# An attention and mixture-of-experts kernel: logits summed from PSUM, rows of x evicted without them

## The chip, the cores and the metric

The kernel runs on one core of a Trainium2 chip. The metric is the device time of one execution in microseconds (us), as the median of several runs. PE is TensorE (PEld its weight loads), DVE is VectorE, ACT is ScalarE, POOL is GpSimd, SP is the engine whose queue issues most DMAs.

## The reference

Attention over 8 batches, 12 heads, 448 tokens and 64 values a head, with the heads mixed before and after the softmax, and behind it a layer of 8 experts (FF = 1024), of which each token takes one:

```python
scores = scale * np.matmul(q, k.transpose(0, 1, 3, 2))
scores = np.einsum('bhij,hg->bgij', scores, w_pre)
scores = scores - np.max(scores, axis=-1, keepdims=True)
attn = np.exp(scores)
attn = attn / (np.sum(attn, axis=-1, keepdims=True) + 1e-09)
attn = np.einsum('bhij,hg->bgij', attn, w_post)
out = np.matmul(attn, v)                 # -> x, 3584 tokens x 768

logits = x @ w_gate                      # 3584 x 8
expert_idx = np.argmax(logits, axis=1)
# gate_w: the chosen expert's softmax probability
for e in range(E):
    h = np.maximum(x[expert_idx == e] @ w1[e], 0.0)
    out[expert_idx == e] = gate_w * (h @ w2[e])
```

## The kernel before, in words

**Tiles and steps.** The 448 queries of a batch are four tiles T of 120, 120, 120 and 88; there are 32 tiles. A tile is cut into blocks of 20 queries, six for a tile of 120 and five for one of 88, so a batch has 23 blocks and the program 184. The attention stage is a loop over the blocks. One turn is called a step here. What stands in a step is a table: `at(u, stage, what)` puts a piece of work into step u, and `ORDER` (L772) is the order of the stages within a step. Nothing else reorders it: each engine takes its instructions in the order in which the program is written. Waits between engines are put in by the framework wherever two instructions touch the same tile of SBUF or the same PSUM bank and one engine has to wait for the other.

**A step.** `mix` (L301) multiplies a block's scores with the heads' mixing matrix into the two banks `bm`. `maxima` (L307, DVE) takes the row maxima of both, `powers` (L315, ACT) the exponentials and their sums, one bank after the other. In the next step `recip` (L323, L325) and `weigh` (L332, POOL) scale the second mixing matrix, and two steps on `post` (L348) and `evict_p` (L366, L360) make the mixed, transposed attention. Scores of later tiles (`qk` L268, `evict_s` L278) are computed in between, into `bs0` and `bs1`, two tiles of two banks each, and are laid out anew by DMAs on SP (`relayout`, L288, into `sb`), two steps ahead of their `mix`. On ACT there are also the roundings of queries (`split_q`, L146) and of key chunks of the next batch (`split_k`, L120).

**The end of a tile.** When all blocks of a tile are mixed, `av` (L388, L408) multiplies with v. `rows` (L428) turns the result into rows of tokens: for each half of the heads, three matmuls against `xg`, whose 136 columns are an identity (128) and the 8 columns of `w_gate` that belong to those 128 values. The outcome is 120 tokens x 3 x 136 values in one bank of `bs1`: 128 values of x and 8 partial logits, three times. The second half fills the other bank. In the next step `evict_r` (L435, ACT) copies both to `XR` in SBUF. One step later `choose` (L455) sums the six partial logits of each expert from `XR` and takes the largest (L459, L460), and `store_x` (L442) writes the rows to `XD` in DRAM, in two halves. Then `mark`, `rank`, `gate` (L500), `place` (L507 to L519) and `scatter` put the token into its expert's list.

**Where these steps stand.** Counted from a batch's first step as 0, `evict_r` stands in the steps 2, 8, 14 and 20, for the tile whose `rows` were in the step before; key chunks of the next batch are rounded in the steps 8, 10, 12, 14, 16 and 18 of the first seven batches. `place` of the tile before stands in the same steps as `evict_r`, on DVE, in the stage "vec". In `ORDER` "vec" comes behind "recip" and ahead of "evict_r", "early" (the key chunk) and "max".

**The last tiles.** For tiles 30 and 31 the same pieces are written out by hand (L839 to L915), together with the gathering of the first expert's tokens from `XD`. Then come the experts, `hidden` (L1065) and `result` (L1086), over sorted tokens.

Of the kernel before, what the change touches and what calls it, by code (L numbers as in the profile page):

```python
# [8 lines left out]
F32 = mybir.dt.float32  # L9
# [6 lines left out]
AX = mybir.AxisListType  # L16
# [4 lines left out]
HD = H * D  # L21
NT = B * S
NE, FF = 8, 1024
P = 128
IT = 120
# [7 lines left out]
NPAIR = H // 2  # L33
CAP = 512
XG = P + NE
NTILE = B * 4
# [8 lines left out]
def attn_moe_kernel(ctx, tc, qT, kT, v, w_pre, w_post, w_gate, w1, w2, out):  # L45
    nc = tc.nc
# [4 lines left out]
    XD = dram.tile([NT + 1, HD], F32, name="XD")  # L51
# [6 lines left out]
    geom = []  # L58
    for T in range(NTILE):
        it = T % 4  # L60
        ni = min(IT, S - it * IT)
# [25 lines left out]
    sm_p = att.enter_context(tc.tile_pool(name="smp", bufs=4))  # L87
    pt_p = att.enter_context(tc.tile_pool(name="ptp", bufs=2))
    x_p = att.enter_context(tc.tile_pool(name="xp", bufs=1))
# [5 lines left out]
    bank_s = [ps_s.tile([P, 2, 512], F32, name=f"bs{n}") for n in range(2)]  # L95
# [275 lines left out]
    HOME, SIDE, SHEET = {}, {}, {}  # L371
# [49 lines left out]
    XR, LG, DD = {}, {}, {}  # L421
# [9 lines left out]
    def evict_r(T, g):  # L431
        ni = geom[T][2]
        if g == 0:
            XR[T] = x_p.tile([IT, NPAIR, XG], F32, name="xr", bufs=2)
        nc.scalar.copy(out=XR[T][:ni, 3 * g:3 * g + 3, :], in_=SHEET.pop((T, g)))  # L435

    def store_x(T, halves=(0, 1)):
        b, it, ni = geom[T][:3]
        t0 = b * S + it * IT
        for n in halves:  # L440
            cs = slice(3 * n, 3 * n + 3)
            nc.sync.dma_start(  # L442
                out=XD[1 + t0:1 + t0 + ni, n * HD // 2:(n + 1) * HD // 2].rearrange("t (c x) -> t c x", x=P),
                in_=XR[T][:ni, cs, :P])

    state = {"base": base0}
    RK = slice(0, NE), slice(NE, 2 * NE)
# [3 lines left out]

    def choose(T):
        b, it, ni = geom[T][:3]
        lg = sm_p.tile([IT, NE], F32, name="lgs")
        nc.vector.reduce_sum(out=lg[:ni], in_=XR[T][:ni, :, P:XG].rearrange("p c e -> p e c"),  # L455
                             axis=AX.X)
        m8 = sm_p.tile([IT, NE], F32, name="m8")
        i8 = sm_p.tile([IT, NE], U32, name="i8")
        nc.vector.max(out=m8[:ni], in_=lg[:ni])  # L459
        nc.vector.max_index(out=i8[:ni], in_max=m8[:ni], in_values=lg[:ni])  # L460
        DD[T] = (lg, m8, i8)
# [150 lines left out]
    def turn(sl, banks, T=None):  # L612
        for ks, bank in zip(KS, banks):
            for n, k in enumerate(range(ks.start, ks.stop)):
                nc.tensor.matmul(out=bank[:, n * P:(n + 1) * P],  # L615
                                 lhsT=XX["s"][:, sl, k * P:(k + 1) * P], rhs=ident,
                                 start=(T is None or n == 0), stop=(T is None), is_transpose=True)
        if T is None:
            return
        ni, hit = geom[T][2], XX["hit", T][:, (sl - 2) * P:(sl - 1) * P]  # L620
        for ks, bank in zip(KS, banks):
            for n, k in enumerate(range(ks.start, ks.stop)):
                nc.tensor.matmul(out=bank[:, n * P:(n + 1) * P], lhsT=XR[T][:ni, k, :P],
                                 rhs=hit[:ni], start=False, stop=(k == ks.stop - 1))

    def split_x(sl, banks):
# [38 lines left out]
    def at(u, stage, *what):  # L665
        steps.setdefault((u, stage), []).append(what)
# [13 lines left out]
    for T in range(NTILE):  # L680
        u0, n = ustart[T], len(geom[T][3])
# [8 lines left out]
    for T in range(NTILE):  # L690
        b, it, ni = geom[T][:3]
        u0, n = ustart[T], len(geom[T][3])
        if T > 1:
            up = ustart[T - 2]
            at(up, "load", load_q, T)
            for part in range(2):
                at(up + 1 + 2 * part, "split", split_q, T, part)
        for g in range(3):
            for c in (2 * g, 2 * g + 1):
                if (T, g) in qsteps:  # L700
                    at(qsteps[T, g], "qk", qk, T, c)
                    at(qsteps[T, g], "evict_s", evict_s, T, c)
        if it == 0 and b + 1 < B:
            U = ustart[T + 4]
            for part, k in enumerate((16, 17, 19, 20, 22, 24, 25, 27)):
                at(u0 + k, "load", load_v, b + 1, part)
            for c in range(NPAIR):
                at(U - 18 + 2 * c, "load", load_k, b + 1, c)
                at(U - 15 + 2 * c, "early", split_k, b + 1, c)
        if T + 1 == NTILE:  # L710
            continue
        vs, r = vsteps[T], rsteps[T]
        for groups in ((0, 1),) if vs[0] == vs[1] else ((0,), (1,)):
            at(vs[groups[0]], "av", av_side, T, groups)
            at(vs[groups[0]], "av", av, T, groups)
        for g in range(2):
            at(vs[g], "side", evict_side, T, g)
            at(vs[g] + 1, "vec", evict_x, T, g)
            at(r, "rows", rows, T, g, bank_s[1][:, g, :])
            at(r + 1, "evict_r", evict_r, T, g)  # L720
        near = T + 2 - NTILE
        if near == 0:
            continue
        for n in range(2):
            at(r + 2 + n, "store", store_x, T, (n,))
        if T == EDGE - 2:
            at(r + 2, "choose", choose, T)
            at(r + 2, "choose", mark, T)
            at(r + 3, "rank", rank, T)
            at(r + 3, "gate", gate, T)  # L730
            for do in (place, token, number):
                at(r + 4, "vec", do, T)
            at(r + 5, "scatter", scatter, T)
            continue
        if T == EDGE - 1:
            at(r + 1, "choose", choose, T)
            at(r + 1, "choose", mark, T)
            at(r + 2, "relayout", rank, T)
            at(r + 2, "relayout", gate, T)
            for do in (place, token, number):  # L740
                at(r + 2, "vec", do, T)
            at(r + 2, "early", scatter, T)
            continue
        long = T + 2 < NTILE and len(geom[T + 2][3]) > 5
        at(r + (1 if near == 0 else 2), "choose", choose, T)
        at(r + (1 if near == 0 else 4 if long else 2), "choose", mark, T)
        u = r + 2 if near == 0 else r + 3 if near == -1 else rsteps[T + 1]
        at(u, "rank", rank, T)
        at(u, "gate", gate, T)
        at(u + 1, "vec", place, T)  # L750
        w = 1 if T == LAST else 4 if T + 3 < NTILE and len(geom[T + 3][3]) > 5 else 2
        at(u + w, "token", token, T)
        at(u + w + 1, "number", number, T)
        at(u + w + 1, "scatter", scatter, T)
# [20 lines left out]
    vec, act = nc.vector.tensor_copy, nc.scalar.copy  # L775
# [60 lines left out]
    T = NTILE - 1  # L836
# [6 lines left out]
    nc.vector.memset(bank_m[0][JC:, W3], 0.0)  # L843
    run(NU, "evict_r")
    store_x(T - 1)
    choose(T - 1)
    mark(T - 1)
# [3 lines left out]
    post(*final, banks=bank_m)  # L851
    rank(T - 1)
    turn(0, side)
    run(NU, "evict_p")
    evict_p(*final, banks=bank_m)
# [23 lines left out]
    logits(T, 0)  # L879
    rows(T, 0, bank_s[1][:, 0, :])  # L880
    evict_r(T, 0)
    logits(T, 1)
    choose_at_once(T)
    mark(T)
    rows(T, 1, bank_s[1][:, 1, :])
    evict_r(T, 1)
    rank(T)
    gate(T)
    turn(1, side)
    place(T)  # L890
    store_x(T)
    nslot = const.tile([P, NE], F32, name="nslot")
    sidx = const.tile([P, NE], I32, name="sidx")
# [11 lines left out]
    number(T)  # L905
    scatter(T)
    turn(2, bank_p, T)
    split_x(2, bank_p)
    turn(3, bank_m, T)
# [246 lines left out]
```

## Time and profile before

| | us |
|---|---|
| three timed runs: median (lowest to highest) | 1260.34 (1255.17 to 1269.69) |
| the profiled execution: time | 1248.09 |
| its span from first to last instruction | 1246.4 |
| PE busy in the span | 1208.5 |
| DVE busy | 774.1 |
| ACT busy | 683.1 |
| POOL busy | 384.2 |

The span is that of the only core. The attention stage takes the first 680 us or so, the experts' stage begins at 708.39. Matmuls are pipelined and the ends of their rows are modelled, so a PE that is busy all the time by its rows can still be waiting a little.

### The profile page before, as it was taken

To read this page: it belongs to the slowest core of one execution; us is meant where nothing else is said; L and a number is where in the kernel's file an instruction comes from. 1 tells how busy PE (TensorE), PEld (TensorE's weight loads), DVE (VectorE), ACT (ScalarE), POOL (GpSimd) and SP (SyncE) were. 2 spreads that over 40 slices of the span, in tenths; PEclk is the share of its full clock that TensorE was granted. 3 is DMA by queue.
4 is the path that set the end of the run, shared out by engine and by line. 5 is a ranking of instruction groups with operands and counts; after the bars stand their busy time and mean duration, and the time that the engine had idled before them with its cause. 6 is when DMAs were issued, how large, how long until landed. Compare 5 with 4: busy or idle time off the path is not lost. (4 is left out here: it accounts for less than half of the span.)

```text
span 1246.4 us, 46562 instructions
## 1 busy us (share of the span) xinstructions
PE 1208.5 (97%) x19601; PEld 1010.6 (81%) x19601; DVE 774.1 (62%) x1964; ACT 683.1 (55%) x1485; POOL 384.2 (31%) x613
## 2 busy tenths in 40 slices
PE   7999999999999999999998799999999999999996
PEld 3677777777777777777776798898989899989886
DVE  5787878878878788778787553424434243434320
ACT  5786878777868787868675342423333242423220
POOL 5443544544535445345335211020201101010000
PEclk9999999999999999999999999999999999999998
DMA  7667557666576676665746364442625344444210
GB/s 207 193 169 207 182 167 212 198 169 208 164 199 198 168 209 199 160 205 169 209 148 192 86 224 154 141 139 89 200 79 173 114 140 145 158 146 140 89 39 33
DMA packets 134858, 200.20 MB, mean 161 GB/s; under 512 B 41637, under 2 KB 112309, under 8 KB 134632
## 3 DMA queue, kind: packets, MB, share of 16 engines
q1 hardware_dynamic: 128438, 172.91, 46.6%
q0 software_dynamic: 6064, 23.86, 5.7%
q8 instruction: 166, 2.72, 0.9%
q14 instruction: 60, 0.49, 0.1%
q10 hardware_dynamic: 130, 0.22, 0.0%
HBM read 97.59 MB, written 23.07 MB: 97 GB/s over the span
## 5 line engine op out<-in xcount | busy, mean ns | idle before, releaser
L315 ACT ACTIVATE et<-bm,st 124x448 f32<-124x448 f32 x360 | 225.2, 631 | 149.5 <-DVE st L307 123.7
L348 PEld LDWEIGHTS bp<-wp,et 60*64 60x64 f32 (+1 forms) x10052 | 197.1, 135 | 75.1 <-issue 52.0
L307 DVE TENSOR_REDUCE st<-bm 124x1 f32<-124x448 f32 x360 | 208.3, 619 | 73.0 <-PE bm L301 66.5
L1065 PE MATMUL pm_h<-si,ah 128*128 128x512 f32 (+1 forms) x768 | 231.5, 382 | 3.6 <-DVEq L1023 2.5
L366 DVE COPY pt<-bp 128x480 f32<-128x480 f32 x352 | 213.4, 647 | 8.1 <-PE bp L348 4.7
L332 POOL TENSOR_SCALAR wp<-Wpost,st 124x60 f32<-124x60 f32 x360 | 150.9, 434 | 170.4 <-DVE st L325 129.3
L348 PE MATMUL bp<-wp,et 60*64 60x60 f32 (+1 forms) x10052 | 191.7, 218 | 4.7 <-issue 4.3
L301 PE MATMUL bm<-sb,Wquad 60*60 60x448 f32 (+3 forms) x1408 | 186.2, 560 | 4.6 <-ACT et L315 4.3
L1065 PEld LDWEIGHTS pm_h<-si,ah 128*128 128x128 f32 x768 | 142.8, 188 | 30.7 <-issue 4.6
L278 ACT COPY si<-bs 120x896 f32<-120x896 f32 (+1 forms) x187 | 159.7, 909 | 10.0 <-PE bs L268 9.2
L1095 POOL DMA_INDIRECT out<-y,ti x30 | 31.9, 1065 | 422.2 <-ACT y L1093 236.7
L1065 PE MATMUL pm_h<-si,al 128*128 128x512 f32 (+1 forms) x384 | 145.5, 379 | 0.0
L1069 DVE SCALAR_TENSOR_TENSOR hl<-pm_h,hh 128x512 fp32r<-128x512 f32 (+1 forms) x64 | 42.1, 658 | 155.8 <-ACT hh L1068 155.7
L408 PE MATMUL bs<-pt,vt 128*64 128x120 f32 (+1 forms) x2496 | 131.7, 260 | 2.6 <-issue 1.3
L1068 ACT ACTIVATE hh<-pm_h 128x512 fp32r<-128x512 f32 (+1 forms) x64 | 36.6, 572 | 177.5 <-PE pm_h L1065 168.8
L408 PEld LDWEIGHTS bs<-pt,vt 128*64 128x64 f32 x2496 | 118.8, 137 | 7.9 <-issue 2.7
L1086 PE MATMUL pm_y<-bh,hh 128*128 128x384 f32 x480 | 124.4, 340 | 0.0
L1086 PE MATMUL pm_y<-bh,hl 128*128 128x384 f32 x480 | 122.0, 335 | 0.0
L1086 PE MATMUL pm_y<-bl,hh 128*128 128x384 f32 x480 | 121.8, 334 | 0.0
L147 POOL TENSOR_TENSOR ql<-qr,qh 128x360 fp32r<-128x360 f32 (+1 forms) x78 | 70.0, 908 | 163.5 <-ACT qh L146 128.4
L1093 ACT ACTIVATE y<-pm_y,tb 128x384 f32<-128x384 f32 x30 | 17.4, 582 | 145.8 <-PE pm_y L1086 87.4
L1091 DVE TENSOR_SCALAR y<-pm_y,tb 128x384 f32<-128x384 f32 x30 | 18.5, 615 | 115.3 <-PE pm_y L1086 115.3
(169 smaller groups left out, 1782.1 us busy)
## 6 DMA issues: line engine op xcount, KB each, us to landing
sb<-si SPq DMA_DIRECT2D x343, 210.0 KB
wraw<-in_w SPq DMA_DIRECT2D x48, 512.0 KB
wraw<-in_w SPq DMA_DIRECT2D x64, 384.0 KB
vt<-in_v SPq DMA_DIRECT2D x64, 192.0 KB
kr<-in_kT SPq DMA_DIRECT2D x42, 224.0 KB
qr<-in_qT SPq DMA_DIRECT2D x48, 180.0 KB
XD<-xr SPq DMA_DIRECT2D x48, 180.0 KB
sb<-si SPq DMA_DIRECT2D x16, 189.0 KB
```

Source lines behind the costliest of these rows:

```text
L147: engine.tensor_sub(out=lo, in0=src, in1=hi.bitcast(F32))
L278: copy(out=SI[T][:ni, 2 * c:2 * c + 2, :], in_=bank[:ni, :, :S])
L301: nc.tensor.matmul(out=bank_m[r][CUT[c], :S], lhsT=Wquad[CUT[r], CUT[c]], rhs=sb[CUT[r], c, :], start=True, stop=True)
L307: nc.vector.reduce_max(out=st[:R1, 0, c:c + 1], in_=bank_m[c][:R1, :S], axis=AX.X, negate=True)
L315: nc.scalar.activation(out=et[:R1, c, :], in_=bank_m[c][:R1, :S], func=AF.Exp, bias=st[:R1, 0, c:c + 1], scale=1.0, accum_out=st[:R1, 1, c ...
L332: nc.gpsimd.tensor_scalar(out=wp[:R1, c, :], in0=Wpost[:R1], scalar1=st[:R1, 2, c:c + 1], scalar2=None, op0=ALU.mult)
L348: nc.tensor.matmul(out=banks[r][col * JC:(col + 1) * JC, at_:at_ + W], lhsT=et[CUT[r], n, kg * JC:(kg + 1) * JC], rhs=wp[CUT[r], n, :], st ...
L366: nc.vector.tensor_copy(out=flat[:, :, i0 + r * IB:i0 + (r + 1) * IB] .rearrange("p x (n k) -> p x n k", k=IQ), in_=banks[r][:, :2 * NJ * ...
L408: nc.tensor.matmul(out=HOME[T, g][r * D:(r + 1) * D, p, :], lhsT=VV[b][:, c, h * D:(h + 1) * D], rhs=PT[T][:, c, h, :ni], start=(c == 0), ...
L1065: nc.tensor.matmul(out=ph[:, :n], lhsT=wx[:, fs], rhs=xx, start=(m == 0), stop=(m == 3 * NK1 - 1))
L1069: nc.vector.scalar_tensor_tensor(out=hl[:, ft, :n], in0=ph[:, :n], scalar=0.0, in1=hh[:, ft, :n].bitcast(F32), op0=ALU.max, op1=ALU.subtract)
L1086: nc.tensor.matmul(out=py[g][:, :384], lhsT=hx[:, kt, ts], rhs=wx[:, g * 384:(g + 1) * 384], start=(n == 0), stop=(n == 3 * NK2 - 1))
```

## The change

The logits are no longer evicted with the rows of x. `evict_r` copies only the 128 values of x of each of the three groups, so `XR` is dense, and a half row of x is one run of 3 x 128 values. The store writes it as one piece of 1536 bytes for each token, where it was three of 512 bytes. The logits are summed by a new function, `add_logits`, straight from the two banks in which `rows` left them. It is placed in the step of `evict_r`, in the stage "vec", ahead of it; for tile 30 in the stage "evict_r", behind it. `choose` takes the sum that is already there.

```diff
     def evict_r(T, g):
         ni = geom[T][2]
         if g == 0:
-            XR[T] = x_p.tile([IT, NPAIR, XG], F32, name="xr", bufs=2)
-        nc.scalar.copy(out=XR[T][:ni, 3 * g:3 * g + 3, :], in_=SHEET.pop((T, g)))
+            XR[T] = x_p.tile([IT, NPAIR, P], F32, name="xr", bufs=2)
+        nc.scalar.copy(out=XR[T][:ni, 3 * g:3 * g + 3, :], in_=SHEET.pop((T, g))[:, :, :P])
+
+    def add_logits(T):
+        ni = geom[T][2]
+        LG[T] = sm_p.tile([IT, NE], F32, name="lgs")
+        parts_ = bank_s[1][:ni, :, :3 * XG].rearrange("p g (c x) -> p x g c", x=XG)[:, P:]
+        nc.vector.reduce_sum(out=LG[T][:ni], in_=parts_, axis=AX.XY)
 
     def store_x(T, halves=(0, 1)):
...
             nc.sync.dma_start(
-                out=XD[1 + t0:1 + t0 + ni, n * HD // 2:(n + 1) * HD // 2].rearrange("t (c x) -> t c x", x=P),
-                in_=XR[T][:ni, cs, :P])
+                out=XD[1 + t0:1 + t0 + ni, n * HD // 2:(n + 1) * HD // 2],
+                in_=XR[T][:ni, cs, :].rearrange("t c x -> t (c x)"))
...
     def choose(T):
         b, it, ni = geom[T][:3]
-        lg = sm_p.tile([IT, NE], F32, name="lgs")
-        nc.vector.reduce_sum(out=lg[:ni], in_=XR[T][:ni, :, P:XG].rearrange("p c e -> p e c"),
-                             axis=AX.X)
+        lg = LG.pop(T)
...
             at(r, "rows", rows, T, g, bank_s[1][:, g, :])
             at(r + 1, "evict_r", evict_r, T, g)
+        at(r + 1, "vec" if T + 2 != NTILE else "evict_r", add_logits, T)
```

How this moves the instructions is shown at two places. `bs_102` and `bs_103` are `bs0` and `bs1`, `bm_104` and `bm_105` the two banks of the mix; in brackets stand the engines and DMA queues whose semaphores an instruction waits for. The numbers of the lines behind L435 grow by a few with the change.

ACT in the step that evicts the first tile's rows and also rounds a key chunk; before:

```order
L146 CAST qh<-qr 128x3x12x10 [waits DMAHW4_49,DMAHW3_49]
L435 COPY xr<-bs_103 120x408 [waits PE_49]
L435 COPY xr<-bs_103 120x408
L120 CAST kh<-kr 128x448 [waits DMAHW0_49]
L315 ACTIVATE et,st<-bm_104,st 124x448 [waits DVE_49,Activation_49]
L315 ACTIVATE et,st<-bm_105,st 124x448 [waits DVE_49]
```

and now:

```order
L146 CAST qh<-qr 128x3x12x10 [waits DMAHW4_49,DMAHW3_49]
L435 COPY xr<-bs_103 120x384 [waits DVE_49]
L435 COPY xr<-bs_103 120x384
L120 CAST kh<-kr 128x448 [waits DMAHW0_49]
L315 ACTIVATE et,st<-bm_104,st 124x448 [waits DVE_49,Activation_49]
L315 ACTIVATE et,st<-bm_105,st 124x448 [waits DVE_49]
```

The order is the same. The first eviction waits for DVE where it waited for PE.

DVE in the step that evicts the second tile's rows, with `place` of the first tile; before:

```order
L323 TENSOR_SCALAR st<-st 124x2 [waits Activation_49]
L325 RECIPROCAL st<-st 124x2 [waits DVE_49]
L507 TENSOR_TENSOR pos<-bs_102,base_128 120x8 [waits PE_49]
L509 TENSOR_TENSOR pos<-pos,ohb 120x8 [waits DVE_49]
L511 TENSOR_REDUCE sc<-pos 120x1 [waits DVE_49]
L515 CAST di<-sc 120x1 [waits DVE_49]
L519 TENSOR_TENSOR nbase<-bs_102,base_128 128x8
L307 TENSOR_REDUCE st<-bm_104 124x1 [waits PE_49,Pool_49]
L307 TENSOR_REDUCE st<-bm_105 124x1 [waits PE_49]
```

and now:

```order
L323 TENSOR_SCALAR st<-st 124x2 [waits Activation_49]
L325 RECIPROCAL st<-st 124x2 [waits DVE_49]
L511 TENSOR_TENSOR pos<-bs_102,base_128 120x8 [waits PE_49]
L513 TENSOR_TENSOR pos<-pos,ohb 120x8 [waits DVE_49]
L515 TENSOR_REDUCE sc<-pos 120x1 [waits DVE_49]
L519 CAST di<-sc 120x1 [waits DVE_49]
L523 TENSOR_TENSOR nbase<-bs_102,base_128 128x8
L441 TENSOR_REDUCE lgs<-bs_103 120x8 [waits PE_49]
L307 TENSOR_REDUCE st<-bm_104 124x1 [waits PE_49,Pool_49]
L307 TENSOR_REDUCE st<-bm_105 124x1 [waits PE_49]
```

The logits' sum (L441) stands between `place` and the maxima. The one that `choose` made, a step later, is gone.

## Rows read from the trace of the kernel before

**Rows 1.** Attention stage: stretch, length, busy us of PE, PEld, DVE, ACT, POOL, clock, DMA, GB/s.

```profile
30.00:680.00 650.00, 639.46 (x16299) 501.69 (x16298) 536.50 (x1587) 491.07 (x1174) 297.57 (x509) 1.00 0.65 188
```

**Rows 2.** Waits, 60 to 680 us: who waited for whom, total us, times, longest us.

```profile
ACT et L315 <- DVE st L307: 114.1, 138, 2.7
DVE st L307 <- PE bm L301: 59.4, 134, 1.0
...
ACT qh L146 <- DMA qr<-in_qT: 2.7, 3, 1.3
...
PEld bm L301 <- DMA sb<-si: 0.2, 1, 0.2
```

**Rows 3.** Timeline, a step with a key chunk: start us, us, engine, line, tiles, count [idle before].

```profile
151.66 0.98 PE L301 MATMUL bm<-sb,Wquad 64*64 64x448 f32 x8
...
152.13 0.93 ACT L435 COPY xr<-bs 120x408 f32<-120x408 f32 x2
...
152.33 0.15 DVE L515 CAST di<-sc 88x1 int32<-88x1 f32 x1
152.40 0.15 DVE L519 TENSOR_TENSOR nbase<-bs,nbase 128x8 f32<-128x8 f32 x1
...
152.96 0.57 ACT L120 CAST kh<-kr 128x448 fp32r<-128x448 f32 x1
...
153.49 0.63 ACT L315 ACTIVATE et<-bm,st 124x448 f32<-124x448 f32 x1
...
154.05 0.37 PE L268 MATMUL bs<-kh,qh 64*88 64x448 f32 x2
154.11 0.63 ACT L315 ACTIVATE et<-bm,st 124x448 f32<-124x448 f32 x1
...
154.46 0.37 PE L268 MATMUL bs<-kh,ql 64*88 64x448 f32 x2
...
154.76 1.09 PE L301 MATMUL bm<-sb,Wquad 64*64 64x448 f32 x8
```

**Rows 4.** Timeline, a step without a key chunk.

```profile
173.62 0.94 ACT L435 COPY xr<-bs 120x408 f32<-120x408 f32 x2
...
173.89 0.16 DVE L519 TENSOR_TENSOR nbase<-bs,nbase 128x8 f32<-128x8 f32 x1
174.22 1.16 DVE L307 TENSOR_REDUCE st<-bm 124x1 f32<-124x448 f32 x2 [0.18 <-PE bm L301]
174.94 0.63 ACT L315 ACTIVATE et<-bm,st 124x448 f32<-124x448 f32 x1 [0.39 <-DVE st L307]
```

**Rows 5.** Timeline, two steps in which something else is late.

```profile
357.60 0.83 ACT L146 CAST qh<-qr 128x360 fp32r<-128x360 f32 x1 [1.27 <-DMA qr<-in_qT]
...
546.33 0.44 PE L348 MATMUL bp<-wp,et 60*64 60x60 f32 x11 [1.73 <-issue]
```

**Rows 6.** Short DVE instructions by line: count, ns shortest/median/longest, first and last start, forms.

```profile
L455 DVE TENSOR_REDUCE lgs<-xr x31: 225/229/241, 74.0 to 686.9; 120x8 f32<-120x48 f32 x24, 88x8 f32<-88x48 f32 x7
...
L459 DVE MAX8 m<-lgs x31: 165/170/172, 74.3 to 687.2; 120x8 f32<-120x8 f32 x24, 88x8 f32<-88x8 f32 x7
...
L360 DVE COPY pt<-bp x14: 336/382/425, 107.7 to 606.0; 128x240 f32<-128x240 f32 x7, 128x192 f32<-128x192 f32 x7
...
L474 DVE MAX8 m<-bm x1: 171/171/171, 698.1 to 698.1; 88x8 f32<-88x8 f32 x1
```

**Rows 7.** Timeline of the tail: a read of a bank behind another.

```profile
701.06 0.15 DVE L519 TENSOR_TENSOR cbase<-bs,nbase 128x8 f32<-128x8 f32 x1
...
701.30 0.37 ACT L630 CAST si<-bs 128x256 fp32r<-128x256 f32 x1 [1.27 <-DVE cbase L519]
```

**Rows 8.** Timeline of the tail: the logits' sum of tile 30.

```profile
686.88 0.24 DVE L455 TENSOR_REDUCE lgs<-xr 120x8 f32<-120x48 f32 x1 [0.72 <-ACT xr L435]
```

More of the change, by code (lines that the diff above doesn't have):

```diff
@@ L622, in turn @@
             for n, k in enumerate(range(ks.start, ks.stop)):
-                nc.tensor.matmul(out=bank[:, n * P:(n + 1) * P], lhsT=XR[T][:ni, k, :P],
+                nc.tensor.matmul(out=bank[:, n * P:(n + 1) * P], lhsT=XR[T][:ni, k, :],
                                  rhs=hit[:ni], start=False, stop=(k == ks.stop - 1))
```

## The prediction, made before the change was run

> **What bounds the kernel now.** I read the stage table first. It splits the 1246.4 us into a short start, the attention stage (30 to 680 us), and a tail and experts' stage that the change hardly enters. In the attention stage PE is busy for 639 of 650 us [rows 1], at a granted clock of 1.00. That does not make PE the bound of every step, since the ends of matmuls are modelled. So I read next who waits for whom in that stage [rows 2]: the exponentials of ACT wait for the maxima of DVE 138 times, and the maxima wait for the mixing matmul 134 times. This is a ring: mix (PE), maxima (DVE), exponentials (ACT), then the next mix, which overwrites the same two banks. Then I read single steps on the timeline. In the step that begins at 151.66 the second exponential ends at 154.11 + 0.63 = 154.74 and the next mix starts at 154.76 [rows 3]. Its length, 3.10 us, is the ring's and not PE's. Steps with much other PE work are longer (mostly 3.4 to 6.3 us); there the ring has slack.
>
> The change works in one step of each tile: the one after `rows`, in which ACT evicts the two sheets. Thirty of the 32 tiles have it in the attention stage or at its end; nearly all of these steps are of the ring-bound kind.
>
> **The change, part by part.**
>
> *The new wait.* Before, the eviction waited for the matmuls alone. Now the logits' sum is written ahead of it and reads the same two banks, and the eviction's first instruction waits for DVE (the ACT rows among the order rows). So the eviction starts after the sum, and behind it on ACT, in order, stand the rounding of a key chunk (in some steps) and the two exponentials of the ring. That a read by ACT waits for a read by DVE of the same bank is already to be seen before the change: the cast at 701.30 had waited 1.27 us for L519, which ends at 701.21, and comes 0.09 us behind it [rows 7]. I use that 0.09 as the hop. [...]
>
> A step with a key chunk [rows 3]: DVE has the reciprocals and five instructions of `place` first; the last, L519, ends at 152.55. An independent DVE instruction starts about 0.08 us before the end of the one in front (L515 ends at 152.48, L519 starts at 152.40), so the sum starts at 152.47. With 0.23 us it ends at 152.70, and the evictions start at 152.79 instead of 152.13: 0.66 us later. They are shorter by 24 of 408 columns, at most 0.05 us of the pair's 0.93; I take 0.04. Remaining: 0.62 us. ACT had no slack: the key rounding ended at 153.53 and the exponential had started at 153.49. So both exponentials, and the next mix, come 0.62 us later.
>
> A step without a key chunk [rows 4]: L519 ends at 174.04, the sum runs from 173.96 to 174.19, the evictions start at 174.28 instead of 173.62, again 0.62 us later net. But ACT had been idle for 0.39 us before its exponential, and the same small overlap adds 0.05. Remaining: 0.18 us.
>
> The count: key chunks of the next batch are rounded in the steps 8, 10, ... 18 of a batch's 23, evictions stand in the steps 2, 8, 14 and 20; so two of four meet, in seven batches, less the one before the first tile's: 13 steps. One of these is the first tile's, without `place` (0.1 us), and one is covered by a PE stall of 1.73 us that comes right behind [rows 5]; 11 are left at 0.60 to 0.66. Of the others eight lose 0.17 to 0.25, four about 0.28, and three nothing, since ACT was late there anyway: its cast had waited up to 1.27 us for a load of q [rows 5]. The last tiles lose nothing. Sum: 11 x 0.62 + 0.1 + 8 x 0.19 + 4 x 0.28 = **9.6 us**. None of it comes back: the step behind is bound by PE's own work, which starts with the late mix.
>
> *The sum's own price* is not in the trace, since no reduction there reads PSUM in such a pattern. The nearest row is the old reduction of the same 48 values from SBUF, 0.23 us [rows 6]; I take that. Below: 0.17, what an instruction on 8 columns takes (L459) [rows 6], which gives 8.1 us in all. Above: 0.34, a copy of 192 columns out of PSUM in broken runs (L360) [rows 6], which gives 12.3 us. Reading from PSUM instead of SBUF shows no price in the trace: the same MAX8 takes 0.17 from either (L474, L459) [rows 6]. [...]
>
> *DVE ahead of the maxima.* The sum also stands between `place` and the maxima, where DVE was idle for 0.18 us [rows 4]. With the overlap it is 0 to 0.1 us too long; that delay lies under the one of ACT, which I have counted.
>
> *What is taken away later.* `choose` loses its reduction, 31 x 0.23 = 7 us of DVE. It stood ahead of steps in which the maxima then wait for the mix [rows 2]; I take nothing. If all of it were on the path, the total would be 2.5.
>
> *Stores.* A half store has 120 pieces of 1536 bytes instead of 360 of 512. What waits for transfers in the stage is 0.2 us for `sb` and 2.7 us for `qr` [rows 2], so the gain is between nothing and 2.9; I take nothing. The stores are issued up to 0.7 us later, and nothing in the stage reads them soon.
>
> *PE* issues the same matmuls. The scores' matmul that next writes the second bank starts at 154.05 [rows 3]; the evictions would end at 152.79 + 0.89 = 153.68, 0.37 us earlier: covered.
>
> *The tail.* For tile 30 the sum stands behind the evictions and reads what they read, so it waits for ACT as its predecessor did, for 0.72 us [rows 8]. Nothing changes.
>
> **The rivals.**
>
> *Longer.* The sum takes 0.35 us or more, or the late eviction also holds up the scores' matmul. From 0.35 on the loss is 12.6 us, over 1%; at 0.5 it is 16.5. For it: 48 values of stride 136, in three dimensions, are farther from any row than the others. Against: all short DVE rows here lie between 0.14 and 0.23.
>
> *Not slower.* The delay falls into time in which PE had work. PE's rows leave no gap at the end of the step: the last scores' matmul ends at 154.83, after the next mix has started [rows 3]. If that end is true, PE and not the ring sets the step, the shift of up to 0.66 us falls on waiting that costs nothing, and what is left is nothing to -2.9 us from the transfers. It decides if PE's spare time in the step is over the shift. Against: with the modelled end left out, matmul pairs there start every 0.2 us, so PE was done at about 154.66, 0.1 us early; and steps of the same work never get shorter than 3.1.
>
> *Faster.* Transfers bound more than the waits show, because 14,336 packets fewer are issued. It would need 12.5 us out of 2.9 that are visible.
>
> **The numbers.** The profiled execution took 1248.09 us; with 9.6 it is 1257.7, +0.77%. But it lies 1% under the median of the three timed runs, 1260.34, and under their lowest, 1255.17. So I add the loss to the mean of the four, 1258.3: **1268 us**. Chances: the forecast 0.60, longer 0.17 (1275 at 0.5 us), not slower 0.20 (1255 to 1258), faster 0.03. The range takes in the bounds 8.1 and 12.3, the case without a loss and the longer one, and a few us of scatter above it: 1254 to 1281. Two medians of this kernel tell 1% from no change, hardly less. The forecast lies below that with 0.48 of its 0.60; with the longer case the chance of slower by over 1% is 0.27, of no change 0.70, of faster 0.03.
>
> **What would show it.** In the changed kernel's trace the first eviction of a pair should be released by the logits' sum; the sum should take about 0.23 us and start right behind the last instruction of `place`. The steps with a key chunk should last 3.7 us instead of 3.1, those without 3.3, with the mix still starting within 0.1 us of the second exponential. The experts' stage should last the same 538 us. I am wrong if the steps keep their 3.1 us, if the sum takes over 0.35 us, or if the loss stands in other steps.

## The result, and the profile after

The changed kernel took 1267.25 us as the median of 22 runs (1255.25 to 1273.45); the kernel before, run beside it on the same chip, 1259.38 (22 runs, 1248.73 to 1269.69). The ratio is 1.0066, with a 95% interval from 1.0041 to 1.0091: 8.3 us slower, between 5.2 and 11.5. That is under the 1% that I had set as the bound of no change. The changed kernel was timed twice more in the experiments, with ratios of 1.0005 and 0.9998; how these go together with the first stands further down. The ratios and their intervals, and the means given further down, leave out executions that took over 1.5% longer than the fastest of the same kernel, while the medians of the tables take in every run, so a ratio is not the quotient of two medians.

The profiled execution of the changed kernel took 1255.67 us, with a span of 1254.0, so it lies 7.6 us above the one of before. The experts' stage starts at 714.63 instead of 708.39, 6.2 us later, and lasts 539.3 us instead of 538.0. So the time is in the attention stage. Its row of the stage table [rows 1], with the same columns:

```profile
30.00:680.00 650.00, 641.35 (x16186) 500.61 (x16184) 528.92 (x1569) 488.45 (x1168) 294.76 (x505) 1.00 0.64 186
```

PE looks as full as before. That DVE, ACT and POOL are less busy is mostly not less work: the same 650 us hold less of the program now (16186 matmuls instead of 16299), and over the whole execution DVE's busy time fell by 3.7 us only (770.4 after 774.1). So this view shows a loss, but not where it is. The waits of 60 to 680 us show more (who waited for whom, total us, times, longest us), the changed kernel:

```profile
ACT et L315 <- DVE st L307: 104.5, 103, 2.9
...
PEld bm L301 <- ACT et L315: 14.3, 42, 0.7
ACT xr L435 <- DVE lgs L441: 13.0, 25, 2.5
...
ACT qh L146 <- DMA qr<-in_qT: 2.2, 2, 1.4
```

The third line is new: in 25 tiles the eviction waits for the logits' sum. The second is the end of its way. The same line of the kernel before reads

```profile
PEld bm L301 <- ACT et L315: 4.6, 14, 0.7
```

so the mix is put down as waiting for the exponentials 28 times more often, 9.7 us in all. Not all of that is new idle time, as the next rows show. What waits for transfers of queries has hardly moved (2.2 us against 2.7 in [rows 2]).

A step with a key chunk, the timeline of the changed kernel (start us, us, engine, line, tiles, count, and in brackets the idle time before it and who ended it). It answers to [rows 3], and by chance it stands at the same time of the span:

```profile
151.67 0.98 PE L301 MATMUL bm<-sb,Wquad 64*64 64x448 f32 x8
...
152.42 0.15 DVE L523 TENSOR_TENSOR nbase<-bs,nbase 128x8 f32<-128x8 f32 x1
...
152.49 0.19 DVE L441 TENSOR_REDUCE lgs<-bs 120x8 f32<-120x48 f32 x1
152.72 0.86 ACT L435 COPY xr<-bs 120x384 f32<-120x384 f32 x2 [0.36 <-DVE lgs L441]
...
153.47 0.58 ACT L120 CAST kh<-kr 128x448 fp32r<-128x448 f32 x1
...
153.93 0.65 ACT L315 ACTIVATE et<-bm,st 124x448 f32<-124x448 f32 x1
...
154.48 0.37 PE L268 MATMUL bs<-kh,ql 64*88 64x448 f32 x2
154.55 0.64 ACT L315 ACTIVATE et<-bm,st 124x448 f32<-124x448 f32 x1
...
154.78 0.19 PEld L301 LDWEIGHTS bm<-sb,Wquad 64*64 64x64 f32 x4 [0.34 <-ACT et L315]
...
155.34 0.19 PEld L301 LDWEIGHTS bm<-sb,Wquad 60*64 60x64 f32 x4 [0.37 <-ACT et L315]
...
155.77 0.54 PE L301 MATMUL bm<-sb,Wquad 60*64 60x448 f32 x2
...
159.40 0.98 PE L301 MATMUL bm<-sb,Wquad 64*64 64x448 f32 x8
```

The sum stands behind the last instruction of `place` and the eviction starts 0.59 us later than before (0.66 had been forecast). But the next mix does *not* start later: 154.78 minus 151.67 is 3.11 us, as before. It starts while the second exponential (to 155.19) is still running. What happens then is in the two weight loads. The mix has two halves, one for each of the two banks `bm`. The first half needs only the first exponential (done at 154.58) and PE itself, and starts in time; in the kernel before, too, the weight loads stood idle for 0.34 us before it, where the profile calls it "issue" (154.75, `[0.34 <-issue]`). The second half needs the second exponential: its weight load waits 0.37 us for ACT and comes at 155.34, and its last matmuls run at 155.77. In the kernel before all eight stood in one group [rows 3]. But in that group too the second half was already released by the second exponential:

```profile
154.63 0.20 ACT L315 ACTIVATION_READ_ACCUMULATOR et<-bm,st 124x1 f32 x1
...
154.88 0.19 PEld L301 LDWEIGHTS bm<-sb,Wquad 60*64 60x64 f32 x4
```

ACT reads out the exponential's sum until 154.83, and the second half's weights follow 0.05 us behind, 0.12 us behind those of the first half (in all eleven steps of this kind it is 0.09 to 0.13). So there was no room left: the second exponential comes 0.44 us later in its step, and the second half 0.44 us later in its group. So the loss appears in the step *behind*: from 154.78 to 159.40 are 4.62 us. Before, that step began at 154.76 and ended with this row:

```profile
158.94 0.98 PE L301 MATMUL bm<-sb,Wquad 64*64 64x448 f32 x8
```

That is 4.18 us. I took all eleven such pairs (the step of the eviction and the one behind it) of the prediction's list by the starts of their mixes: 80.1 us in the kernel before, 85.1 in the changed one. Before, each pair took 7.28 us; now they take 7.72 to 7.79. In the median the second exponential ends 3.08 us after the start of its own mix before, and 3.52 after.

A step without a key chunk. The mix of the step in [rows 4] is this row of the kernel before:

```profile
173.11 0.98 PE L301 MATMUL bm<-sb,Wquad 64*64 64x448 f32 x8
```

and the same step of the changed kernel:

```profile
173.27 0.98 PE L301 MATMUL bm<-sb,Wquad 64*64 64x448 f32 x8
...
174.12 0.20 DVE L441 TENSOR_REDUCE lgs<-bs 120x8 f32<-120x48 f32 x1
174.35 0.86 ACT L435 COPY xr<-bs 120x384 f32<-120x384 f32 x2 [0.36 <-DVE lgs L441]
...
175.10 0.64 ACT L315 ACTIVATE et<-bm,st 124x448 f32<-124x448 f32 x1
...
175.73 0.63 ACT L315 ACTIVATE et<-bm,st 124x448 f32<-124x448 f32 x1
```

The exponential starts 1.83 us after its mix, before and after (174.94 in [rows 4]). The 0.39 us that ACT had been idle there took the delay; steps like this one lose nothing by it. In three others (a batch's third step) the eviction starts later in the step, the second exponential comes 0.10 to 0.19 us later than before, and the pair of steps grows by as much (6.90 us to 7.00, 7.00 and 7.09): 0.4 us in all.

Sum, eviction and store by their lines (count, ns shortest/median/longest, first and last start, forms), the changed kernel:

```profile
L441 DVE TENSOR_REDUCE lgs<-bs x31: 185/196/209, 67.8 to 693.1; 120x8 f32<-120x48 f32 x24, 88x8 f32<-88x48 f32 x7
L435 ACT COPY xr<-bs x64: 462/479/525, 68.0 to 705.4; 120x384 f32<-120x384 f32 x48, 88x384 f32<-88x384 f32 x16
L448 SPq DMA_DIRECT2D XD<-xr x64: 283/510/1497, 68.5 to 705.9; - x64
```

and of the kernel before the last of the three:

```profile
L442 SPq DMA_DIRECT2D XD<-xr x64: 283/508/1624, 68.6 to 699.8; - x64
```

In the tail the sum of tile 30 waits for ACT as its predecessor did [rows 8], 0.69 us instead of 0.72:

```profile
693.06 0.21 DVE L441 TENSOR_REDUCE lgs<-bs 120x8 f32<-120x48 f32 x1 [0.69 <-ACT xr L435]
```

### The profile page after: what moved, and what is told of

It reads as the page before. It is cut to its first block, busy times and chain, and to the rows that moved or that the text cites. A ratio compares the mean times of both kernels' runs of the same rounds, so it can differ in the third digit from the quotient of the medians.

```text
span 1254.0 us, 46593 instructions
## 1 busy us (share of the span) xinstructions
PE 1216.0 (97%) x19601; PEld 1015.6 (81%) x19601; DVE 770.4 (61%) x1964; ACT 682.2 (54%) x1485; POOL 384.4 (31%) x613
## 2 busy tenths in 40 slices
DMA packets 120522, 200.20 MB, mean 160 GB/s; under 512 B 41637, under 2 KB 97973, under 8 KB 120296
## 5 line engine op out<-in xcount | busy, mean ns | idle before, releaser
L348 PEld LDWEIGHTS bp<-wp,et 60*64 60x64 f32 (+1 forms) x10052 | 200.4, 135 | 72.5 <-issue 51.9
L348 PE MATMUL bp<-wp,et 60*64 60x60 f32 (+1 forms) x10052 | 196.6, 219 | 3.5 <-issue 3.4
L301 PE MATMUL bm<-sb,Wquad 60*60 60x448 f32 (+3 forms) x1408 | 192.0, 562 | 4.5 <-ACT et L315 4.5
L301 PEld LDWEIGHTS bm<-sb,Wquad 60*60 60x60 f32 (+3 forms) x1408 | 45.9, 129 | 55.2 <-issue 24.1
```

What stands on the lines that cost most here:

```text
L301: nc.tensor.matmul(out=bank_m[r][CUT[c], :S], lhsT=Wquad[CUT[r], CUT[c]], rhs=sb[CUT[r], c, :], start=True, stop=True)
L348: nc.tensor.matmul(out=banks[r][col * JC:(col + 1) * JC, at_:at_ + W], lhsT=et[CUT[r], n, kg * JC:(kg + 1) * JC], rhs=wp[CUT[r], n, :], st ...
```

## The experiments

The theory, W: the loss is the wait of the eviction for the sum, because the sum stands behind `place` and ahead of a key chunk's rounding; it costs about 0.45 us in 11 steps. The rivals: D, the sum's own time on DVE ahead of the maxima; S, the dense eviction and the larger pieces of the stores. Every kernel was timed against runs of the kernel before on its chip, in three sessions of four kernels each, in the order of the table's last twelve rows; the medians of the kernel before there are 1263.05 (34 runs), 1265.04 (35) and 1264.35 (35). "Pairs" is the sum over the eleven pairs of steps in the profiled execution, "second exp" the median end of the second exponential after its mix in steps with and without a key chunk (the latter without steps that something else delays). In some traces a few pairs are held up by something else, which raises the sum; the median pair tells the kernels apart more sharply: 7.28 us before, 7.72 to 7.76 where the eviction waits for one sum, 8.04 with two sums, and 7.28 to 7.30 in all the others.

| kernel | median us (runs) | ratio to before (95%) | pairs us | second exp us |
|---|---|---|---|---|
| before, profiled | | | 80.1 | 3.08 / 3.08 |
| changed, profiled | 1267.25 (22) | 1.0066 (1.0041 to 1.0091) | 85.1 | 3.52 / 3.09 |
| sum first | 1255.21 (12) | 0.9974 (0.9942 to 1.0006) | 81.0 | 3.09 / 3.09 |
| sum only | 1260.02 (12) | 1.0006 (0.9973 to 1.0038) | 85.7 | 3.56 / 3.13 |
| sum twice | 1266.39 (11) | 1.0056 (1.0026 to 1.0085) | 88.2 | 3.85 / 3.39 |
| key first | 1254.27 (12) | 0.9963 (0.9933 to 0.9993) | 80.9 | 3.09 / 3.09 |
| sum first, sparse | 1257.78 (12) | 0.9976 (0.9934 to 1.0019) | 81.8 | 3.09 / 3.09 |
| sum and key first | 1257.24 (12) | 0.9973 (0.9933 to 1.0014) | 81.1 | 3.09 / 3.09 |
| sum last | 1257.36 (12) | 0.9961 (0.9924 to 0.9998) | 81.8 | 3.08 / 3.08 |
| changed, second session | 1262.05 (12) | 1.0005 (0.9967 to 1.0043) | 85.6 | 3.55 / 3.10 |
| before, as a control | 1257.28 (12) | 0.9991 (0.9957 to 1.0026) | 80.8 | 3.08 / 3.08 |
| changed, third session | 1259.76 (12) | 0.9998 (0.9959 to 1.0037) | 85.6 | 3.55 / 3.09 |
| sum first, third session | 1256.63 (12) | 0.9979 (0.9944 to 1.0014) | 80.8 | 3.09 / 3.09 |
| sum last, third session | 1258.76 (12) | 0.9998 (0.9961 to 1.0035) | 81.5 | 3.08 / 3.08 |

**Sum first.** The sum is written ahead of `place`; DVE does the same work, and only its order changes.

```diff
-        at(r + 1, "vec" if T + 2 != NTILE else "evict_r", add_logits, T)
+        at(r + 1, "recip" if T + 2 != NTILE else "evict_r", add_logits, T)
```

> The changed kernel with the logits' sum moved ahead of place on DVE (behind the reciprocals); everything else as changed. Theory W (the loss is ACT's wait for a sum that stands behind five instructions of place): the evictions start within 0.1 us of where they started before the change, the steps that follow a step with a key chunk go back from about 4.62 us to 4.15, and the time is that of the kernel before, ratio 0.998 to 1.003. Theory D (the loss is the sum's own time on DVE ahead of the maxima): the sum is still ahead of the maxima, so the ratio stays at 1.005 to 1.008.

The wait is almost gone. In the stage's waits of this kernel, two are left:

```profile
ACT xr L435 <- DVE lgs L441: 2.1, 2, 1.8
```

and the pairs are back at 81.0. The same step in its repetition, from the third session:

```profile
153.93 0.98 PE L301 MATMUL bm<-sb,Wquad 64*64 64x448 f32 x8
154.04 0.21 DVE L441 TENSOR_REDUCE lgs<-bs 120x8 f32<-120x48 f32 x1
...
154.41 0.89 ACT L435 COPY xr<-bs 120x384 f32<-120x384 f32 x2
...
155.20 0.57 ACT L120 CAST kh<-kr 128x448 fp32r<-128x448 f32 x1
...
156.39 0.63 ACT L315 ACTIVATE et<-bm,st 124x448 f32<-124x448 f32 x1
...
157.04 1.08 PE L301 MATMUL bm<-sb,Wquad 64*64 64x448 f32 x8
...
161.22 0.98 PE L301 MATMUL bm<-sb,Wquad 64*64 64x448 f32 x8
```

The sum is done at 154.25, the eviction starts at 154.41 after ACT's own work, all eight matmuls stand in one group again, and the step behind takes 4.18 us. The sum still takes its 0.2 us of DVE ahead of the maxima, and nothing is lost: D falls. The ratio, 0.9974, came out just under W's range.

**Sum only.** The kernel before, with `add_logits` in the same place as in the change and `choose` taking its sum, but with evictions of 408 columns and stores in pieces of 512 bytes:

```diff
-        lg = sm_p.tile([IT, NE], F32, name="lgs")
-        nc.vector.reduce_sum(out=lg[:ni], in_=XR[T][:ni, :, P:XG].rearrange("p c e -> p e c"),
-                             axis=AX.X)
+        lg = LG.pop(T)
...
+        at(r + 1, "vec" if T + 2 != NTILE else "evict_r", add_logits, T)
```

> The kernel before with the logits' sum alone taken from PSUM, at the same place as in the changed kernel; evictions of 136 columns and stores in pieces of 512 bytes stay. Theory W: as slow as the changed kernel, ratio 1.005 to 1.008, with the same steps of 4.62 us. Theory S (the dense eviction or the longer pieces of the stores cost the time): ratio 0.998 to 1.002.

Without anything of the dense rows the pairs are 85.7, as in the changed kernel: the loss is the sum's. The ratio, 1.0006, is not W's; it lies in the range given for S. But against the two kernels of the same session in which the eviction is not held up to any effect (sum first, key first), this one is 5.7 us slower by the means of the runs, with an estimate of 2.5 to 8.8 from their scatter. What makes the ratio small is told below, with the control.

**Sum twice.** The sum's cost by itself, doubled:

```diff
+        for _ in range(2 if T + 2 < NTILE else 1):
             nc.vector.reduce_sum(out=LG[T][:ni], in_=parts_, axis=AX.XY)
```

> The changed kernel with the sum issued twice in a row for each tile but the last two (0.2 us more of wait and of DVE). Theory W: the steps behind a key chunk's step grow by another 0.2 us, from 4.62 to about 4.8, 13 x 0.2 = 2.6 us, and the steps behind the others grow by 0 to 0.2, 0 to 3 us: ratio 1.009 to 1.011, with the maxima less than 0.3 us later. Theory D: every step with a sum grows by 0.2 us itself, 28 x 0.2 = 5.6 us, ratio 1.011 or more, with the time in the same step and not in the one behind.

A step with a key chunk, the kernel with two sums:

```profile
324.53 0.98 PE L301 MATMUL bm<-sb,Wquad 64*64 64x448 f32 x8
...
325.35 0.43 DVE L442 TENSOR_REDUCE lgs<-bs 120x8 f32<-120x48 f32 x2
...
325.87 0.86 ACT L435 COPY xr<-bs 120x384 f32<-120x384 f32 x2 [0.65 <-DVE lgs L442]
...
327.08 0.65 ACT L315 ACTIVATE et<-bm,st 124x448 f32<-124x448 f32 x1
...
327.70 0.64 ACT L315 ACTIVATE et<-bm,st 124x448 f32<-124x448 f32 x1
327.87 0.19 PEld L301 LDWEIGHTS bm<-sb,Wquad 64*64 64x64 f32 x4 [0.57 <-ACT et L315]
```

The second exponential moves by another 0.3 us, and the pairs by 3.1 (0.28 us each). It does not come where I had expected it: the step with the eviction itself grows, here from about 3.10 to 3.34 us and in ten of the eleven to between 3.34 and 3.46, because now the first exponential (to 327.73) ends later than PE's own work, and the whole mix waits. The step behind takes 4.67, where it took 4.60 to 4.66 with one sum. And the steps without a key chunk, most of which had room for one sum, have none for two: their second exponential ends 3.39 us after the mix instead of 3.09, and the steps behind them grow by about 0.3. The mix is put down as waiting for the exponentials 59 times, 21.5 us in all. So the second sum's time appears in the step itself where there is a key chunk, which W had not expected, and in the step behind where there is none; the ratio, 1.0056, is below both ranges.

**Key first.** The rounding of a key chunk, which needs nothing of the sum, goes ahead of the eviction on ACT:

```diff
-             "evict_r", "early", "max", "number", "exp", "post", "rank", "av", "rows", "gate", "evict_p",
+             "early", "evict_r", "max", "number", "exp", "post", "rank", "av", "rows", "gate", "evict_p",
```

> The changed kernel with the rounding of the key chunk ahead of the evictions on ACT, so that it runs while ACT would wait. Theory W: in the steps with a key chunk the wait of 0.36 us before the evictions is filled, the exponentials come about 0.2 us earlier than in the changed kernel, and the steps behind shrink from 4.62 to about 4.4: 2 to 3 us of the loss go, ratio 1.003 to 1.005. Theory D: no change, 1.005 to 1.008.

```profile
154.41 0.98 PE L301 MATMUL bm<-sb,Wquad 64*64 64x448 f32 x8
154.88 0.58 ACT L120 CAST kh<-kr 128x448 fp32r<-128x448 f32 x1
...
155.23 0.20 DVE L441 TENSOR_REDUCE lgs<-bs 120x8 f32<-120x48 f32 x1
155.46 0.86 ACT L435 COPY xr<-bs 120x384 f32<-120x384 f32 x2
...
156.24 0.64 ACT L315 ACTIVATE et<-bm,st 124x448 f32<-124x448 f32 x1
...
157.52 1.08 PE L301 MATMUL bm<-sb,Wquad 64*64 64x448 f32 x8
```

The sum is as late as in the change, and the pairs are at 80.9 all the same: the rounding lies in the time in which ACT would have waited. I had expected about half of the loss back and it was all of it. This is the sharpest stroke against D and S, as neither DVE's work nor the stores differ from the changed kernel. It also shows that the eviction's lateness costs nothing by itself: it starts 1.05 us behind its mix, as in the changed kernel. What counts is when the exponentials come.

**Sum first, sparse; sum and key first.** The first is "sum only" with "recip" for "vec" in the line of `add_logits`; the second has the edits of "sum first" and "key first".

> The kernel before with the logits' sum from PSUM ahead of place; evictions of 136 columns and stores in pieces of 512 bytes as before. Theory W: no loss in the steps behind the key chunks (4.15 us), ratio 0.997 to 1.001. Theory S (dense evictions and pieces of 1536 bytes matter by themselves): it differs by over 0.3% from the changed kernel with the sum first, which gave 0.9974.

> The changed kernel with the sum ahead of place and the key chunk ahead of the evictions, a candidate for the best version. Theory W: with the sum first there is no wait left to fill, so the key chunk's place gives nothing more: 0.995 to 1.000, as with the sum first alone.

Against "sum first", the sparse form shows what the dense rows and 1536-byte stores are worth: 0.9976 against 0.9974 and 0.9979, nothing that these runs can show, though their intervals of 0.4% to either side would hide a small effect; the median pair is 7.29 us in both. With "sum only" and "key first", S falls as the cause of the loss in the pairs. Both orders together gain nothing over either.

**Sum last.** The sum behind the eviction and the maxima, so that DVE waits for ACT's read and not ACT for DVE's ("number" in place of "vec").

> The changed kernel with the sum behind the two maxima of its step, so that it waits for the evictions and they wait for PE alone. Theory W: evictions and exponentials are back where they were before the change (second exponential 3.1 us after the mix), the steps behind at 4.15 us; but the matmul of the scores that next writes the second bank now waits for the sum, 0 to 0.2 us in up to 28 steps: ratio 0.998 to 1.004. Theory D (the sum's time on DVE costs wherever it stands): 1.004 or more.

```profile
152.77 0.98 PE L301 MATMUL bm<-sb,Wquad 64*64 64x448 f32 x8
...
153.25 0.89 ACT L435 COPY xr<-bs 120x384 f32<-120x384 f32 x2
...
154.96 0.20 DVE L441 TENSOR_REDUCE lgs<-bs 120x8 f32<-120x48 f32 x1
...
155.23 0.63 ACT L315 ACTIVATE et<-bm,st 124x448 f32<-124x448 f32 x1
...
155.99 0.98 PE L301 MATMUL bm<-sb,Wquad 64*64 64x448 f32 x8
...
160.06 0.98 PE L301 MATMUL bm<-sb,Wquad 64*64 64x448 f32 x8
```

No eviction waits for the sum. The scores' matmuls, which next write the bank, now wait for the sum (27 times, 9.8 us), so the step is 3.22 us; but the step behind is 4.07, and the pair takes 7.29, as in the kernel before. The sums of 81.8 and 81.5 in the table come from a few pairs that something else held up (one of 8.91 us in the first trace). The ratio, 0.9961, is below both ranges.

**The repetitions and the control.**

> The changed kernel again, beside the next three and against the same runs of the kernel before. Theory W (evictions wait for a sum that stands behind place; in the trace about 0.45 us in the step behind each of 13 key-chunk steps, some 6 us): ratio 1.003 to 1.008, the second exponential of a key-chunk step ends 3.5 us after its mix. If the first measurement's 1.0066 held more than that (a cost of the dense rows or of the longer pieces), it stays above 1.006 and the next kernel, with neither, comes out under the changed kernel with the sum first.

> The kernel before itself, timed as if it were a new one: what this comparison shows of no change at all. If the 0.3% by which the kernels without the wait came out under the kernel before is real, this gives 0.999 to 1.001; if it comes from the way of comparing, it gives 0.996 to 0.998 as well.

> The changed kernel a third time, beside the kernel before as a new one. Theory W: 4 to 6 us (0.3 to 0.5%) over c0_before_again and over the next two; the 11 pairs of a key-chunk step and the step behind add up to about 85 us in its trace.

> The changed kernel with the sum ahead of place, again. Theory W: within 0.2% of c0_before_again and 0.3 to 0.5% under c1_changed_again; the 11 pairs add up to about 81 us.

> The changed kernel with the sum behind the maxima, again. Theory W: like c2_sum_first_again, 0.3 to 0.5% under c1_changed_again; the 11 pairs add up to 81 to 82 us.

The trace repeats: 85.6 and 85.6 for the changed kernel, 80.8 for the kernel before. The times do so less, and most of what had been expected of them did not come: the changed kernel's ratios are 1.0066, 1.0005 and 0.9998, and the interval of the last lies wholly below that of the first. In the third session the changed kernel is 2.5 us above the control in the median and 3.1 and 1.0 above the two others, where 4 to 6 us had been expected.

The control shows one reason why the ratios of the experiments say little: timed as a new one, the kernel before took 1257.28 us in the median, and the runs of it that stood beside the new kernels 1264.35. So the new kernels are better compared with each other. The eviction waits for one sum in "sum only" and in the changed kernel of the second and third session (35 runs); in the other kernels but "sum twice", the control among them, it costs nothing in the traces (91 runs). The means are 1261.5 and 1257.4, 4.1 us apart, with an estimate of 2.3 to 5.9 from the scatter of the single runs. By sessions it is 5.7, 5.1 and 1.8 us, and the last of these is not clear of nothing. That agrees with the 5 us of the pairs. The rest of the 8.3 us of the first comparison did not come back in the later two; it stays open. No version is shown to be faster than the kernel before: two intervals end just under 1 (0.9993 and 0.9998), but the second of them did not repeat (0.9998, with an interval to 1.0035), and the control's own ratio is 0.9991. What is shown, by the pairs in the traces, is that sum first, key first and sum last take the loss away.

## Why the prediction was right, and where it was not

- *The time:* 1268 was forecast and 1267.25 measured, slower by less than 1%. Part of that closeness is luck: the loss on the path was forecast as 9.6 us, and the traces show 5. The changed kernel's later medians, 1262.05 and 1259.76, lie 6 and 8 us below the forecast, though within its range. The chances at the end of the prediction don't add up as given: what is left of the forecast above 1% (0.12) and the longer case (0.17) make 0.29 and not 0.27.
- *The new wait:* right. The eviction is released by the sum, 25 times, 13.0 us.
- *Where the loss appears: wrong.* "So both exponentials, and the next mix, come 0.62 us later" failed in its last part, and by the prediction's own test ("I am wrong if the steps keep their 3.1 us") it failed. The step that failed is the reading that the second exponential, which ended 0.02 us ahead of the next mix [rows 3], released the whole mix. It released the second half alone, 0.12 us behind the first; the first half, which did not move though both exponentials came 0.44 us later, starts as far as the rows show when PE's own work is done. The rival "not slower" had this half right, PE does set the mix's start; what neither saw is that the mix's second half has a wait of its own, for the second bank, and that the lateness is paid there and turns up in the step behind (4.18 us to 4.62).
- *The price of a step with a key chunk:* 0.62 forecast, 0.45 measured (5.0 us over 11 pairs). In the step shown, the sum took 0.19 and not 0.23 us; ACT came 0.04 us behind it (152.68 to 152.72) and not 0.09; the pair of evictions became 0.07 shorter, not 0.04. These are 0.12 us. The rest is slack that the forecast had put at nothing: the first exponential started 0.53 us after the rounding of the key chunk before (152.96 to 153.49 in [rows 3]) and 0.46 now (153.47 to 153.93).
- *The steps without one:* 2.6 us forecast, about 0.4 measured, in three steps. In the others the evictions start 0.57 us later in the step (1.08 us after the mix at 173.27, against 0.51 after the one at 173.11) and end 0.49 later. ACT's idle 0.39 us [rows 4] covered most of this, and the exponential now starts 0.11 us before the evictions' end (175.10 against 175.21), where 0.05 had been taken; so it comes as early as before.
- *The sum's price:* the nearest row (0.23) was the better guide than the dearer bound (0.34). The sum out of PSUM took 196 ns in the median, less than the 229 of the one out of SBUF [rows 6]. The two sums also differ in the pattern in which they read, so no run shows what the memory alone makes of it.
- *The two readers of a bank:* in each of the 25 waits the eviction starts 0.03 to 0.04 us behind the end of the sum and not beside it. The wait itself was written into the program by the framework; what two reads at once would do, no run here shows.
- *What was costed at nothing:* right for `choose`'s reduction, for the stores and for the tail (0.69 us against 0.72). The rivals "longer" and "faster" did not happen.
- *The experts' stage:* 539.3 us instead of 538.0, with nothing changed in it; I count that and the rest outside the pairs as differences between executions. In the attention stage other steps moved both ways: one with late queries from 3.30 to 3.99 us, one with a stall of PE from 5.16 to 3.50, while the step behind that one grew from 4.20 to 5.37.

## What to carry to other kernels

A second reader of a PSUM bank can cost the first one a wait (here 25 waits, 13.0 us); put the short reader as far ahead as its data allow, or move work of the waiting engine that doesn't need it into the wait: either took the whole loss of the pairs away here (81.0 and 80.9 us, against 85.1 in the changed kernel and 80.8 in the control). When a start coincides with an end in a trace, look for the instruction that was really released by it: here a group of matmuls over two banks was released bank by bank (154.78 and 155.34), and the gap hid inside the group. A sum over the steps of interest shows such a loss where the length of a single step doesn't. And a doubled cost shows how much room a step had: one sum was hidden in most of the steps without a key chunk (second exponential 3.09 us after the mix), two were not (3.39).

## What the runs showed of the hardware

The sum of 48 values took 196 ns out of PSUM, in a pattern of three dimensions, against 229 out of SBUF [rows 6]. The pieces of the stores became a third as many, and the whole program's packets fell from 134,858 to 120,522, but the issue of a store on SP took 510 ns in the median, after 508, and no run became measurably shorter by it (sum first against its sparse form, to within 0.4%). In the eleven steps looked at, the weights of the mix's second half followed the read-out of the second exponential by 0.05 us, before the change and after it.
